# Attention and gated feed-forward on one core: the second batch's q and k loaded in runs of six tokens and transposed by TensorE

## The chip, the cores and the metric

The kernel runs on one core of a Trainium2 chip. The time is device microseconds of one execution. The kernel before was run eight times: the median is 413.78 us, the lowest 411.63, the highest 416.57.

A core has five engines that work side by side, each through its own instructions in order. TensorE (PE) multiplies matrices out of SBUF into PSUM, VectorE (DVE) and ScalarE (ACT) read PSUM and compute element by element, GpSimd (POOL) computes on SBUF and here also issues nearly all loads, and SyncE (SP) issues DMA transposes and stores.

## What is computed

There are 8 batches, 8 heads, 576 tokens of 64 values per head, and 16 beacon keys and values that every token may attend to. In float32:

```python
k_all = concatenate([beacon_k, k], axis=2)
v_all = concatenate([beacon_v, v], axis=2)
scores = (q @ k_all.T) / 8          # causal over k, open over the beacons
a = softmax(scores)
x = (a @ v_all)                     # to (4608 tokens, 512)
out = (gelu(x @ w_gate) * (x @ w_val)) @ w_out     # d_ff = 1536
```

## The kernel before, in words

**Batches and chunks.** The outer loop goes over the 8 batches. For each, an attention fills 576 columns of `xT_sb` (the transposed x, bf16); then a gate phase (`gate_val`) works on one chunk of 512 tokens: 12 tiles, each of 8 matmuls of 512 columns, a GELU on ACT and a product on DVE. The output product (`o(n)`, n matmuls of 512 columns) is behind by a chunk and is strewn over the next attentions to fill TensorE there. After the last batch a ninth chunk follows.

**Attention.** Heads go in four pairs. Per pair, `scores` makes the transposed scores in four chunks (S0 to S3), each of which ACT turns into exp; the scores' PSUM tile has two buffers (`psum_s`), which the gate phase uses too. `mask` clears what lies above the diagonal, on POOL (affine select) or on DVE by a table. `sums` (Z) makes the row sums and the first 64 columns of the values product, `values` (V) the rest, `invert` (I) the reciprocals on DVE, `scale` (M) writes `xT_sb`. `sums` and `values` have one PSUM buffer each, with the tags z and x; the output product has one with the tag o.

**The order is written out by hand.** `attention(b, *slots)` gets one string per slot; each word emits one step, and `keep` holds the program order on every engine. S, Z, V, I, M are as above, with the pair as the digit; `O12` is twelve matmuls of the output product; `N3` issues the next three loads of a queue (`load_next`); `aMC` and `dMC` mask chunk C of pair M on POOL or DVE; `kMt` and `qMt` transpose pair M through the PSUM bank t.

**How q and k reach TensorE.** q and k must lie transposed in `qkT` (`qk_ring`, two buffers). For batch 0, `load_runs` loads two heads of q or k with six tokens, 1.5 KB, to a piece, and `trans` makes 12 transposes on TensorE per operand and pair (plus one for the beacon keys), which DVE copies from PSUM to `qkT` in the right token order. For batches 1 to 7, `qk_loads` loads 11 row tiles with 256-byte pieces, and at the start of the gate phase before, `xbar_transpose` (lines 161 to 168) puts ten DMA transposes on SP's queue. Attention b+1 starts when they have landed.

**DMA semaphores.** In the built program the loads that POOL issues take eight semaphores in turn: each waits until the load eight places before it has landed.

Of the kernel before, what the change touches and what calls it, by code (L numbers as in the profile page):

```python
# [58 lines left out]
def kernel(  # L59
# [53 lines left out]
    def dma(out_ap, in_ap):  # L113
        keep(nc.gpsimd.dma_start(out=out_ap, in_=in_ap))  # L114

    def load_runs(h0, h1):
        for src, dst in ((q, q6), (k, k6)):
            dma(dst[:, h0:h1, :], src[0, h0:h1, :, :].rearrange("h (p r) d -> p h (r d)", r=RUN))

    def load_rows(start, dst, src, h0, h1):  # L120

# [24 lines left out]
    def qk_loads(b):  # L146

        qt, kt = q_ring[b % 2], k_ring[b % 2]

        def rows(dst, src):  # L150
            return dst.rearrange("p (h d) -> p h d", d=D), src.rearrange("h p d -> p h d")

        loads = [rows(kt[0:NB, 0, :], beacon_k[b])]
        for j in range(5):
            r0, n = (NB, 112) if j == 0 else (0, KROWS[j])
            loads.append(rows(kt[r0 : r0 + n, j, :], k[b, :, S_LO[j] : S_LO[j] + n, :]))
            n = min(P, S - j * P)
            loads.append(rows(qt[0:n, j, :], q[b, :, j * P : j * P + n, :]))
        return loads

    def xbar_transpose(b):
        qt, kt, qkT = q_ring[b % 2], k_ring[b % 2], qk_ring[b % 2]
        for j in range(5):
            n = KROWS[j]
            keep(nc.sync.dma_start_transpose(out=qkT[:, 1, :, j * P : j * P + n], in_=kt[0:n, j, :]))  # L165
            n = P if j < 4 else 64
            c = NB + j * P
            keep(nc.sync.dma_start_transpose(out=qkT[:, 0, :, c : c + n], in_=qt[0:n, j, :]))  # L168
# [4 lines left out]
    def load_v(b):  # L173
        dst = flat(v_ring[b % 2])
        load_beacon(dma, dst[0:NB, 0, :], beacon_v[b])
        load_keyed(dma, dst, v[b], 0, H)
# [12 lines left out]
    def load_out_w():  # L189
        dma(wo_sb, moe_w_out.rearrange("(ii p) m -> p ii m", p=P))  # L190
# [24 lines left out]
        n = in_ap.shape[0]  # L215
        keep(nc.tensor.transpose(out_ap, in_ap, ident[0:n, 0:n]))

    def trans(m, w, t_ps, copies):

        src = (q6, k6)[w]  # L220
        if w:
            tr(t_ps[:, S : S + NB], bk0[:, m * P : (m + 1) * P])
        by_run = t_ps[:, 0:S].rearrange("p (r t) -> p r t", r=RUN)
        for r in range(RUN):
            for hi in range(2):
                tr(by_run[64 * hi : 64 * hi + 64, r, :], src[:, 2 * m + hi, r * D : (r + 1) * D])
        dst = qk_ring[0]
        if w:
            copies[0][1](dst[:, 1, m, 0:NB], t_ps[:, S : S + NB])
        c0 = 0  # L230
        for c1, copy in copies:
            copy(
                dst[:, w, m, NB + c0 : NB + c1].rearrange("p (t r) -> p t r", r=RUN),
                t_ps[:, 0:S].rearrange("p (r t) -> p t r", r=RUN)[:, c0 // RUN : c1 // RUN, :],
            )
            c0 = c1
# [4 lines left out]
    def act_copy(o, i):  # L241
        keep(nc.scalar.copy(o, i))

    def trans_in(tag, m, w, copy=None):
        t_ps = bank(tag, BF16, 1024, "t_ps")
        trans(m, w, t_ps, [(S, copy or dve_copy)])

    exp_of, x_of, z_of = {}, {}, {}

    def scores(b, m, *chunks):  # L250
        i = b * NPAIR + m
        qkT = qk_ring[b % 2]
        for c in chunks:
            if c == 0:
                exp_of[i] = epool.tile([P, 2, EXP_W], BF16, name="expT", tag="expT")
            expT = exp_of[i]
            s_ps = psum_s.tile([P, 2, 512], FP32, name="s_ps", tag="s")
            for t, s_lo, w, col in CHUNKS[c]:
                for hi in range(2):
                    r = slice(64 * hi, 64 * hi + 64)  # L260
                    mm(
                        s_ps[:, hi, col : col + w],
                        qkT[r, 1, m, t * P : (t + 1) * P],
                        qkT[r, 0, m, NB + s_lo : NB + s_lo + w],
                        True,
                        True,
                    )
            o, w = CHUNK_OFF[c], CHUNK_W[c]
            act(expT[:, :, o : o + w], s_ps[:, :, 0:w], ACT.Exp, scale=QK_SCALE)
            if b:  # L270
                mask(b, m, c)

    def mask(b, m, c, by_table=False):
# [110 lines left out]
    def gate_val(ci, f0, f1):  # L384
        for fi in range(f0, f1):
            gate_val_mms(ci, fi, range(K_CHUNKS))
            gate_val_end(ci, fi)
# [13 lines left out]
    def o(n):  # L401
        for _ in range(n):
            ci, u = divmod(out_done[0], OUT_UNITS)
            ti, fi = divmod(u, F_TILES)
            if fi == 0:
                o_ps_of[0] = psum_o.tile([P, D_MODEL], FP32, name="o_ps", tag="o")
            o_ps = o_ps_of[0]
            mm(
                o_ps,
                h_of[ci][:, fi, ti * P : (ti + 1) * P],  # L410
                wo_sb[:, fi, :],
                fi == 0,
                fi == F_TILES - 1,
            )
            if fi == F_TILES - 1:
                o_sb = opool.tile([P, D_MODEL], FP32, name="o_sb", tag="o_sb")
                keep(nc.vector.tensor_copy(o_sb, o_ps))  # L417
                n0 = ci * CH + ti * P
                keep(nc.sync.dma_start(out=out[n0 : n0 + P, :], in_=o_sb))
            out_done[0] += 1  # L420
# [7 lines left out]
    def attention(b, *slots, extra=None):  # L428


        for m, slot in enumerate(slots):
            for step in slot.split():
                kind, n = step[0], step[1:]
                if kind == "S":
                    scores(b, m, *(int(c) for c in n))
                elif kind == "Z":
                    sums(b, int(n or m - 1))
                    if not n:
                        invert(b, m - 1)
                elif kind == "I":  # L440
                    invert(b, int(n))
                elif kind == "V":
                    values(b, int(n or m - 1))
                    if not n:
                        scale(b, m - 1)
                elif kind == "M":
                    scale(b, int(n))
                elif kind == "O":
                    o(int(n))
                else:  # L450
                    extra[kind](*n) if kind in "kqrwLhyad" else extra[kind](n)

# [1 line left out]

    exp_table()
    heat(8)
    load_runs(0, 2)
    load_beacon(dma, bk0, beacon_k[0])
    keep(
        nc.gpsimd.affine_select(  # L460
# [6 lines left out]
            channel_multiplier=1,  # L467
        )
    )
    load_runs(2, 4)  # L470
    keep(
        nc.gpsimd.affine_select(
            out=tri,
# [7 lines left out]
    )  # L481
    for w, copies, n in ((0, [(S, dve_copy)], 0), (1, [(114, act_copy), (S, act_copy)], 1)):
        t0 = psum_s.tile([P, 2048], BF16, name="t0_ps", tag="s")
        trans(0, w, t0, copies)
        heat(n)

    queue = []
# [1 line left out]
    def load_next(n):  # L489
# [2 lines left out]

    W_CUT = ((0, 512), (512, 1024), (1024, 1536))
    extra = {
        "k": lambda m, tag: trans_in(tag, int(m), 1),
        "q": lambda m, tag: trans_in(tag, int(m), 0),
        "a": lambda m, c: mask(0, int(m), int(c)),
        "d": lambda m, c: mask(0, int(m), int(c), by_table=True),
        "r": lambda m: load_runs(2 * int(m), 2 * int(m) + 2),
        "h": lambda n, tag: heat(int(n), tag),  # L500
        "L": lambda: load_out_w(),
        "y": lambda t: load_v_tile(0, int(t)),
        "X": lambda n: load_v(1),
        "N": lambda n: load_next(int(n)),
        "w": lambda i: load_gate_val(*W_CUT[int(i)]),
    }
    queue.extend(qk_loads(1))
    attention(
        0,
        "r2 h3x S0 k1o q1x S1 r3 y2 S2 d00 y0 q2o y1 k2x S3 d02 y3 d01 d03", "S0 y4 S1 w0 Z0 d10 S2 I0 a11 S3 k3x", "a12 S0 q3o S1 S2 a13 V0 M0 Z1 V1 w1 S3", "a21 I1 a20 a23 M1 S0 S1 a22 w2 Z2 V2 I2 S2 S3", "h3o a30 a31 a32 M2 a33 Z3 V3 I3 M3",  # L510
        extra=extra,
    )
    load_next(99)
    load_v(1)
    gelu_table()
    gate_val_first(0, heat, 2, 1)
    xbar_transpose(1)
    gate_val(0, 1, F_TILES)

    for b in range(1, B):  # L520
        exp_table()
        if b + 1 < B:
            queue.extend(qk_loads(b + 1))
        if b == 1:
            attention(b, "L S0 S1 S2 S3 N3", "S0 S1 Z0 S2 I0 S3 V0 N3", "M0 Z1 S0 S1 O7 I1 S2 S3 V1 M1 N3", "S0 S1 Z2 V2 S2 I2 S3 M2 O5 N2", "Z3 I3 V3 M3 O12", extra=extra)
        elif b == 2:
            attention(b, "S0 O12 S1 S2 O12 S3 N3", "S0 Z0 S1 S2 I0 O12 S3 V0 M0 N3", "S0 S1 Z1 V1 S2 S3 O7 N3", "S0 I1 S1 M1 Z2 V2 S2 S3 I2 M2 N2", "O1 O4 Z3 V3 I3 O12 M3", extra=extra)
        else:
            attention(b, "O5 S0 S1 O7 S2 S3 O2 N3", "S0 S1 Z0 I0 V0 S2 M0 S3 O10 N3", "S0 S1 Z1 V1 I1 S2 S3 M1 O12 N3", "S0 S1 Z2 V2 I2 M2 S2 S3 O5 N2", "Z3 I3 V3 M3", extra=extra)
        gelu_table()  # L530
        if b + 1 < B:
            load_next(99)
            load_v(b + 1)
        gate_val_first(b, o, 0 if b == 1 else 0 if b == 2 else 7)
        if b + 1 < B:
            xbar_transpose(b + 1)
        gate_val(b, 1, F_TILES)
# [35 lines left out]
```

## Time and profile before

| | us |
|---|---|
| median of 8 runs | 413.78 |
| the profiled execution's own time | 413.64 |
| its span | 411.9 |
| PE busy (94% of the span) | 387.3 |
| DVE / ACT / POOL busy | 190.9 / 189.2 / 167.9 |

The stages of the first batches, by the chain and the timeline of the profile (us from the span's start):

| stage | start | end |
|---|---|---|
| attention 0 (first scores to first gate matmul) | 7.25 | 28.87 |
| gate phase 0 | 28.87 | 50.69 |
| attention 1 | 50.69 | 78.68 |
| gate phase 1 | 78.68 | 99.49 |
| attention 2 | 99.49 | 124.58 |

From batch 3 on each batch takes 42.8 us. In the profile, L195 is the helper of all matmuls, L198 of all activations, L114 of all loads, L286 the mask on POOL, L165 and L168 the DMA transposes of k and q, L216 the transposes on TensorE, L239 their copies on DVE. PEclk is the granted TensorE clock as a part of full speed.

### The profile page before, as it was taken

To read this page: it belongs to the slowest core of one execution; us is meant where nothing else is said; L and a number is where in the kernel's file an instruction comes from. 1 tells how busy PE (TensorE), PEld (TensorE's weight loads), DVE (VectorE), ACT (ScalarE), POOL (GpSimd) and SP (SyncE) were. 2 spreads that over 40 slices of the span, in tenths; PEclk is the share of its full clock that TensorE was granted. 3 is DMA by queue.
4 is the path that set the end of the run, shared out by engine and by line. 5 is a ranking of instruction groups with operands and counts; after the bars stand their busy time and mean duration, and the time that the engine had idled before them with its cause. 6 is when DMAs were issued, how large, how long until landed. Compare 5 with 4: busy or idle time off the path is not lost.

```text
span 411.9 us, 6523 instructions
## 1 busy us (share of the span) xinstructions
PE 387.3 (94%) x2565; PEld 176.6 (43%) x2565; DVE 190.9 (46%) x326; ACT 189.2 (46%) x255; POOL 167.9 (41%) x301
## 2 busy tenths in 40 slices
PE   7889939999999999999999999999999999999975
PEld 3444314444444444444444344444444444444432
DVE  2673305643474446543664366436634574333321
ACT  3743347335662386337643665357434853312200
POOL 8769229800693049603970198009910420000000
PEclk9789969999999999999999999999999999999999
DMA  7999999990699329960999099918991100001012
GB/s 99 181 184 152 159 156 64 124 148 9 102 108 146 66 36 128 123 110 28 103 131 130 24 98 108 147 27 98 110 150 39 53 28 25 0 27 51 27 52 76
DMA packets 151983, 37.38 MB, mean 91 GB/s; under 512 B 141200, under 2 KB 147344, under 8 KB 151952
## 3 DMA queue, kind: packets, MB, share of 16 engines
q0 software_dynamic: 111824, 19.15, 61.1%
q1 hardware_dynamic: 40128, 17.82, 20.6%
q8 instruction: 20, 0.33, 0.3%
q14 instruction: 11, 0.09, 0.1%
HBM read 38.27 MB, written 9.44 MB: 116 GB/s over the span
## 4 chain that ended last, share of the span: by engine, by line
PE 78%; POOL 6%; DMA 5%; SPq 3%; DVE 3%; issue 2%; ACT 2%; POOLq 0%; DVEq 0%
PE gv_ps L195 40%; PE o_ps L195 21%; PE s_ps L195 6%; PE z_ps L195 6%; PE x_ps L195 5%; DMA qkT<-q_sb 3%; POOL expT L286 2%; DVE o_sb L417 2%; ACT expT L198 2%; SPq L165 2%; DMA k_sb<-in_k_dram 2%; SPq L168 1%; DMA v_sb<-in_v_dram 1%; POOL k_sb L114 1%; POOL q_sb L114 1%
## 5 line engine op out<-in xcount | busy, mean ns | idle before, releaser
L198 ACT ACTIVATE ge_sb<-gv_ps 128x512 bf16<-128x512 f32 x108 | 64.5, 597 | 157.4 <-PE gv_ps L195 157.4
L379 DVE TENSOR_TENSOR hT_sb<-gv_ps,ge_sb 128x512 bf16<-128x512 f32 x108 | 74.7, 692 | 118.0 <-ACT ge_sb L198 118.0
L286 POOL TENSOR_SCALAR_AFFINE_SELECT expT<-expT 128x256 bf16<-128x256 bf16 (+2 forms) x154 | 56.2, 396 | 163.7 <-ACT expT L198 163.5
L198 ACT ACTIVATE expT<-s_ps 128x1024 bf16<-128x1024 f32 (+3 forms) x128 | 103.4, 861 | 41.2 <-PE s_ps L195 38.8
L195 PE MATMUL gv_ps<-xT_sb,wg_sb 128*128 128x512 bf16 x432 | 112.2, 379 | 0.5 <-DVE xT_sb L347 0.5
L195 PE MATMUL gv_ps<-xT_sb,wv_sb 128*128 128x512 bf16 x432 | 112.2, 379 | 0.0
L195 PE MATMUL o_ps<-wo_sb,hT_sb 128*128 128x512 bf16 x432 | 103.5, 380 | 4.0 <-DVE o_sb L417 3.8
L195 PEld LDWEIGHTS <-wv_sb 128*128 128x128 bf16 x432 | 42.3, 98 | 51.8 <-issue 1.1
L195 PEld LDWEIGHTS <-wg_sb 128*128 128x128 bf16 x432 | 41.8, 98 | 51.1 <-issue 1.6
L195 PEld LDWEIGHTS <-hT_sb 128*128 128x128 bf16 x432 | 39.9, 98 | 52.3 <-issue 7.1
L195 PE MATMUL s_ps<-qkT 64*128 64x80 bf16 (+5 forms) x384 | 41.7, 294 | 10.1 <-DMA qkT<-q_sb 6.8
L417 DVE COPY o_sb<-o_ps 128x512 f32<-128x512 f32 x36 | 24.8, 690 | 44.0 <-PE o_ps L195 44.0
L330 DVE STREAM_TRANSPOSE zt<-z_ps 128x576 f32<-128x576 f32 x32 | 25.1, 783 | 41.6 <-PE z_ps L195 41.6
L114 POOL DMA_DIRECT2D v_sb<-in_v_dram x40 | 34.0, 888 | 0.8 <-DMA q_sb<-in_q_dram 0.8
L195 PE MATMUL z_ps<-expT,ones 80*64 80x80 bf16 (+5 forms) x384 | 31.6, 296 | 1.8 <-DVE xT_sb L347 1.4
L195 PEld LDWEIGHTS <-qkT 64*128 64x128 bf16 x384 | 14.8, 96 | 43.0 <-issue 36.0
L114 POOL DMA_DIRECT2D k_sb<-in_k_dram x35 | 29.9, 854 | 1.7 <-DMA wv_sb<-in_moe_w_val_dram 0.9
L114 POOL DMA_DIRECT2D q_sb<-in_q_dram x35 | 30.2, 863 | 0.2
L195 PE MATMUL x_ps<-expT,v_sb 128*64 128x512 bf16 (+4 forms) x320 | 28.8, 311 | 0.0
L335 DVE STREAM_TRANSPOSE rec<-rz 128x576 f32<-128x576 f32 x32 | 24.9, 778 | 1.1
L347 DVE TENSOR_TENSOR xT_sb<-x_ps,rec 128x512 bf16<-128x512 f32 x32 | 21.8, 682 | 3.1 <-PE x_ps L195 3.1
L195 PEld LDWEIGHTS <-ones 128*64 128x64 bf16 (+1 forms) x384 | 16.2, 113 | 15.6 <-issue 8.8
(36 smaller groups left out, 105.2 us busy)
## 6 DMA issues: line engine op xcount, KB each, us to landing
out_dram<-o_sb SPq DMA_DIRECT2D x36, 256.0 KB, 2.4
q_sb<-in_q_dram POOLq DMA_DIRECT2D x28, 128.0 KB, 4.5
v_sb<-in_v_dram POOLq DMA_DIRECT2D x24, 128.0 KB, 5.7
k_sb<-in_k_dram POOLq DMA_DIRECT2D x21, 128.0 KB, 4.9
wg_sb<-in_moe_w_gate_dram POOLq DMA_DIRECT2D x3, 512.0 KB, 6.7
wv_sb<-in_moe_w_val_dram POOLq DMA_DIRECT2D x3, 512.0 KB, 8.5
wo_sb<-in_moe_w_out_dram POOLq DMA_DIRECT2D x1, 1536.0 KB, 18.2
v_sb<-in_v_dram POOLq DMA_DIRECT2D x8, 112.0 KB, 3.7
```

The costliest lines, as they stand in the source:

```text
L114: keep(nc.gpsimd.dma_start(out=out_ap, in_=in_ap))
L165: keep(nc.sync.dma_start_transpose(out=qkT[:, 1, :, j * P : j * P + n], in_=kt[0:n, j, :]))
L168: keep(nc.sync.dma_start_transpose(out=qkT[:, 0, :, c : c + n], in_=qt[0:n, j, :]))
L195: keep(nc.tensor.matmul(out_ap, lhsT, rhs, start=start, stop=stop, **kw))
L198: keep(nc.scalar.activation(out_ap, in_ap, func, **kw))
L286: nc.gpsimd.affine_select(out=d, in_=d, pattern=[[0, 2], [1, DIAG[t]]], compare_op=ALU.is_ge, fill=0.0, base=base, channel_multiplier=-1,)
L330: keep(nc.vector.transpose(zt, z_of[i][:, Z0 : Z0 + S]))
L335: nc.vector.transpose(rec.rearrange("p (n j) -> p n j", j=32), rz.unsqueeze(2).to_broadcast([P, NBLK, 32]))
L347: nc.vector.tensor_tensor(out=xT_sb[:, m, b * S + q0 : b * S + q1], in0=acc[:, 0 : q1 - q0], in1=rec[:, q0:q1], op=ALU.mult,)
L379: nc.vector.tensor_tensor(out=h_of[ci][:, fi, :], in0=gv_ps[:, 1, :], in1=ge_sb, op=ALU.mult)
L417: keep(nc.vector.tensor_copy(o_sb, o_ps))
```

## The change

Batch 1 gets its q and k as batch 0 does. Its loads are `load_runs` pieces (eight, and the beacon keys into `bk0`) instead of eleven row tiles. `xbar_transpose(1)` is gone from gate phase 0. Pair 0 is transposed on TensorE inside gate phase 0: k after tile 6 through the bank z, q after tile 7 through the bank x. Pairs 1 to 3 are transposed inside attention 1. There, the masks are now written out, three chunks of pair 0 on DVE and the rest on POOL. The 24 matmuls of the output product in attention 1 stand at its end (`O12` twice) instead of as `O7`, `O5`, `O12`. Of batch 2's eleven loads three are issued early in attention 1 and eight behind its last mask. `load_v(1)` and `load_out_w()` stand behind gate phase 0 in the program; in POOL's own order they still follow batch 1's q and k loads. Attention 2 keeps its 60 matmuls of the output product, with its steps and loads in another order.

```diff
-    def load_runs(h0, h1):
-        for src, dst in ((q, q6), (k, k6)):
-            dma(dst[:, h0:h1, :], src[0, h0:h1, :, :].rearrange("h (p r) d -> p h (r d)", r=RUN))
+    def runs(b, m):
+        h = slice(2 * m, 2 * m + 2)
+        return [
+            (dst[:, h, :], src[b, h, :, :].rearrange("h (p r) d -> p h (r d)", r=RUN))
+            for src, dst in ((q, q6), (k, k6))
+        ]
+
+    def load_runs(b, m):
+        for out_ap, in_ap in runs(b, m):
+            dma(out_ap, in_ap)
...
-    def trans(m, w, t_ps, copies):
+    def trans(b, m, w, t_ps, copies):
...
-        dst = qk_ring[0]
+        dst = qk_ring[b]
...
-            if b:
+            if b > 1:
                 mask(b, m, c)
...
-    queue.extend(qk_loads(1))
+    queue.extend(runs(1, 0) + [by_token(bk0, beacon_k[1])])
+    for m in range(1, NPAIR):
+        queue.extend(runs(1, m))
...
     load_next(99)
-    load_v(1)
     gelu_table()
     gate_val_first(0, heat, 2, 1)
-    xbar_transpose(1)
-    gate_val(0, 1, F_TILES)
+    gate_val(0, 1, 7)
+    trans_in("z", 1, 0, 1)
+    gate_val(0, 7, 7 + 1)
+    trans_in("x", 1, 0, 0)
+    gate_val(0, 7 + 1, F_TILES)
+    load_v(1)
+    load_out_w()
...
-            attention(b, "L S0 S1 S2 S3 N3", "S0 S1 Z0 S2 I0 S3 V0 N3", "M0 Z1 S0 S1 O7 I1 S2 S3 V1 M1 N3", "S0 S1 Z2 V2 S2 I2 S3 M2 O5 N2", "Z3 I3 V3 M3 O12", extra=extra)
+            attention(b, "S0 S1 k1x a01 q1z S2 k3o d00 S3 d03 d02", "S0 N3 k2o S1 a11 a10 Z0 q2o I0 S2 a12 V0 M0 S3 a13", "S0 S1 q3o a21 Z1 I1 a20 S2 V1 a22 S3 M1", "S0 a23 S1 a30 a31 Z2 S2 I2 V2 a32 M2 S3 a33 O12", "Z3 N3 V3 I3 M3 N3 O12", extra=extra)
         elif b == 2:
-            attention(b, "S0 O12 S1 S2 O12 S3 N3", "S0 Z0 S1 S2 I0 O12 S3 V0 M0 N3", "S0 S1 Z1 V1 S2 S3 O7 N3", "S0 I1 S1 M1 Z2 V2 S2 S3 I2 M2 N2", "O1 O4 Z3 V3 I3 O12 M3", extra=extra)
+            attention(b, "S0 O12 N3 S1 S2 O12 S3 N3", "S0 Z0 I0 S1 S2 O12 S3 V0 N3", "S0 S1 M0 Z1 V1 I1 S2 S3 O7", "S0 S1 M1 Z2 V2 I2 S2 S3 N2 M2", "O2 O3 Z3 I3 V3 M3 O12", extra=extra)
```

More of the change, by code (lines that the diff above doesn't have):

```diff
@@ L114, in dma, with by_token @@
         keep(nc.gpsimd.dma_start(out=out_ap, in_=in_ap))
[L116 to L118 removed]
+    def runs(b, m):
[7 more added lines that the diff above has]
+            dma(out_ap, in_ap)
+    def by_token(dst, src):
+        return dst.rearrange("p (h d) -> p h d", d=D), src.rearrange("h p d -> p h d")
     def load_rows(start, dst, src, h0, h1):
@@ L148, in qk_loads @@
         qt, kt = q_ring[b % 2], k_ring[b % 2]
-        def rows(dst, src):
-            return dst.rearrange("p (h d) -> p h d", d=D), src.rearrange("h p d -> p h d")
-        loads = [rows(kt[0:NB, 0, :], beacon_k[b])]
+        loads = [by_token(kt[0:NB, 0, :], beacon_k[b])]
         for j in range(5):
             r0, n = (NB, 112) if j == 0 else (0, KROWS[j])
-            loads.append(rows(kt[r0 : r0 + n, j, :], k[b, :, S_LO[j] : S_LO[j] + n, :]))
+            loads.append(by_token(kt[r0 : r0 + n, j, :], k[b, :, S_LO[j] : S_LO[j] + n, :]))
             n = min(P, S - j * P)
-            loads.append(rows(qt[0:n, j, :], q[b, :, j * P : j * P + n, :]))
+            loads.append(by_token(qt[0:n, j, :], q[b, :, j * P : j * P + n, :]))
         return loads
@@ L242, in act_copy, with trans_in @@
         keep(nc.scalar.copy(o, i))
-    def trans_in(tag, m, w, copy=None):
+    def trans_in(tag, b, m, w):
         t_ps = bank(tag, BF16, 1024, "t_ps")
-        trans(m, w, t_ps, [(S, copy or dve_copy)])
+        trans(b, m, w, t_ps, [(S, dve_copy)])
     exp_of, x_of, z_of = {}, {}, {}
@@ L449, in attention @@
                     o(int(n))
+                elif kind in "adkq":
+                    extra[kind](b, *n)
                 else:
@@ L456 @@
     heat(8)
-    load_runs(0, 2)
+    load_runs(0, 0)
     load_beacon(dma, bk0, beacon_k[0])
@@ L469 @@
     )
-    load_runs(2, 4)
+    load_runs(0, 1)
     keep(
@@ L483 @@
         t0 = psum_s.tile([P, 2048], BF16, name="t0_ps", tag="s")
-        trans(0, w, t0, copies)
+        trans(0, 0, w, t0, copies)
         heat(n)
@@ L494 @@
     extra = {
[L495 to L499, printed above, removed]
+        "k": lambda b, m, tag: trans_in(tag, b, int(m), 1),
+        "q": lambda b, m, tag: trans_in(tag, b, int(m), 0),
+        "a": lambda b, m, c: mask(b, int(m), int(c)),
+        "d": lambda b, m, c: mask(b, int(m), int(c), by_table=True),
+        "r": lambda m: load_runs(0, int(m)),
         "h": lambda n, tag: heat(int(n), tag),
-        "L": lambda: load_out_w(),
         "y": lambda t: load_v_tile(0, int(t)),
-        "X": lambda n: load_v(1),
         "N": lambda n: load_next(int(n)),
```

## The prediction

> **What bounds the kernel now.** I read the chain of work that ended last first, in order of time. From batch 3 on it is TensorE nearly alone, 42.8 us per batch. Between gate phase 0 and attention 1 it leaves TensorE:
>
> ```profile
> 46.40 1.19 SPq L165
> 47.70 10.35 DMA qkT<-q_sb
> 58.09 0.60 PE s_ps L195 x6
> 58.71 1.81 ACT expT L198 x2
> ```
>
> The ten DMA transposes go out from 34.63 us on, one per 1.4 us, and the last needs 10.35 us to land, beside the load of `wo_sb`. TensorE's timeline shows the hole (start, length, what, and in brackets the idle time before):
>
> ```profile
> 49.66 1.03 PE L195 MATMUL gv_ps<-xT_sb,wv_sb 128*128 128x512 bf16 x4
> 54.23 0.61 PE L195 MATMUL s_ps<-qkT 64*128 64x512 bf16 x2 [3.55 <-DMA qkT<-q_sb]
> 58.09 0.97 PE L195 MATMUL s_ps<-qkT 64*128 64x64 bf16 x8 [3.25 <-DMA qkT<-q_sb]
> 59.73 0.36 PE L195 MATMUL s_ps<-qkT 64*128 64x208 bf16 x2 [0.67 <-ACT expT L198]
> ```
>
> TensorE ends at 50.69, and the second scores start at 58.09: 7.4 us with only 0.6 of work. The clock tells the rest. It changes only at multiples of 3.41 us (near 16.05, 22.88, 53.59 and 63.83), so I asked for busy time by stage in stretches of that length, for TensorE (PE busy, instructions, granted clock, then DMA), and for the transposes on TensorE alone (the first busy column):
>
> ```profile
> 9.22:12.64 3.42, 2.82 (x60) 1.00 1.63 157
> 12.64:16.05 3.41, 1.92 (x31) 1.00 2.13 165
> 16.05:19.46 3.41, 3.24 (x30) 0.50 1.25 204
> 19.46:22.88 3.42, 3.42 (x32) 0.50 1.23 202
> ...
> 57.00:60.42 3.42, 1.33 (x10) 0.50 0.95 157
> 60.42:63.83 3.41, 3.26 (x28) 0.50 0.15 13
> 63.83:67.24 3.41, 2.57 (x36) 1.00 1.12 71
> ```
>
> ```profile
> 9.22:12.64 3.42, 1.24 (x38) 2.98 (x6) 0.00 (x0) 1.00 1.63 157
> 12.64:16.05 3.41, 0.55 (x13) 0.00 (x0) 0.00 (x0) 1.00 2.13 165
> 16.05:19.46 3.41, 0.69 (x12) 1.51 (x3) 0.00 (x0) 0.50 1.25 204
> ```
>
> A stretch 1.92 us busy is followed by half the clock, one 2.57 us busy is not. After the hole the half clock lasts from 53.59 to 63.83. So the wait costs 6.8 us of idle and slows attention 1, which ends at 78.68: 28.0 us for 24 output matmuls at 0.216 us (5.2) and four pairs of exp.
>
> **What the change removes.** The wait for `qkT` goes: no DMA transposes of batch 1 remain (SP has ten fewer). The runs land in time. POOL reaches them at 27.8; eight at 0.69 us and the beacon keys at 0.56 are issued in 6.1 us instead of 9.2. Before, the ninth load waited until 34.4 for the last weights, and the new ninth waits too; pair 0 is issued by 29 and needed near 43. The v loads and `wo_sb` follow earlier than before, and `wo_sb` (43.3, 18.2 us to land) is first read later than now.
>
> **What it adds to gate phase 0.** The groups give a transpose of q a mean of 244 ns and of k 210. A hundred at these means would be 23 us, but the starts overlap: at full clock twelve follow each other in 0.38 us, with the beacon keys 0.47. [...] The row has the pace, so pair 0 costs 0.85 us of TensorE, all on the path: the gate phase ends at 51.5. On DVE a gate tile is 0.69 of product and 1.03 idle; each copy (0.75, for k 0.15 more) stands behind a product and fits the idle time. If it did not, the two buffers of `gv_ps` would hold TensorE; at worst that is one copy, 0.75.
>
> **Attention 1 at full clock, by rows.** The table load after the last GELU ends at 52.62 now, at 53.5 then; four exps of a pair take 3.24.
> Slot 0: exps 53.5 to 56.7; the second scores wait for the last product, near 52.9.
> Slot 1: exps of S0 and S1 to 58.6. DVE has copies of k1, q1, k3 and three masks (0.28 each) until 57.3; Z0 waits for these masks and runs to 58.2, q2 to 58.6, S2 to 58.8. Exps end at 60.1.
> Slot 2: exps of S0 and S1 to 62.0, but Z1 needs the bank z: the q2 copy (0.75), inverses (1.85) and the first scale (0.22) from 58.6 give 61.45. Z1 to 62.3, S2 to 62.5, exps end at 64.0.
> Slot 3: DVE ends the scales at 62.1, the q3 copy at 62.9, inverses and first scale at 65.0; Z2 to 65.9; exps end at 67.5.
> Tail: O12 from 66.9 to 69.5, Z3 0.86, V3 0.69, O12 2.6: gate phase 1 starts at 73.6, 5.1 us earlier than 78.68. POOL is not late: 17 masks at 0.4 and three loads are under 10 us.
>
> **The clock speaks against this sum.** From 51.5 to 57.3 TensorE has five scores groups and five groups of transposes. By the rows (0.35 to 0.39 a scores group, 0.45 a transposing one, ends modelled as in the view) a 3.41 us stretch of it is about 2.1 busy: between the 1.92 that lost the clock and the 2.57 that kept it, nearer the first. [...] I take the drop, near 55 to 57.
>
> Its price: attention 0's half clock lasted two stretches, 6.8 us. Half of that, 3.4, is lost where TensorE is never idle; in the sum above it is idle about a fifth, so 2.7 (three stretches: 5.1 less 1.2, near 3.9). With 2.7 gate phase 1 starts at 76.3, a gain of 2.4; with 3.9 the gain is 1.2; with none 5.1.
>
> **What moves behind it.** Batch 2's last eight loads (0.74 to 0.9 each, some 7 us) follow the last mask on POOL and end about 1.5 us after gate phase 1 has started; they ended 2.2 before it, and the v loads follow. SP's first transpose comes 1.4 after the start anyway (80.11, behind the store of the last output tile) and takes one load per 1.3 us; the ten went out until 93.6, DMA is idle from 96, and attention 2 began at 99.49. So 3.5 us of slack cover this; gone, each microsecond late is one of TensorE, after an O12 of 2.6 that stands before S1.
>
> Attention 2, now 25.1 us, has 60 x 0.216 = 13.0 of output matmuls and about 9 of attention work, so at most 3.1 can go. Near its end the chain runs through POOL: three loads (116.6 to 119.3), masks, then Z3 at 1.43 instead of 0.91; and the gate's last k chunk waits 0.22 for `xT_sb`. The new order puts the loads a slot earlier and the last scale before O12. The first three now stand ahead of S1's masks, but sums wait for S3's mask in any case (106.94), so nothing excludes either sign: -1 to 3.1. I take 0.8, from 0.5 for Z3, 0.2 for the wait and a little from POOL. Batches 3 to 7 do not change.
>
> The sum on the profiled execution: 413.64 - 2.4 - 0.8 = 410.4; the median of the runs is 0.14 above that execution, which I leave out.
>
> **The rivals.**
> - The clock holds. For: 2.1 is not 1.92, and the stretches' phase may cover gate work. [...] 413.64 - 5.1 - 0.8 = 407.7. Chance 0.22.
> - The gain is given back: three slow stretches and nothing in attention 2, 413.64 - 1.2 = 412.4. [...] Chance 0.13.
> - Slower: the half clock holds until the output matmuls. All of them now stand at the end, where before an O7 stood in slot 2. The place is slots 1 to 3: at half clock Z is 1.60 and V 1.48, so Z2 starts near 68.4 and exps end at 72.6; the first O12 at half clock takes 5.2, from 71.9, to about 77; Z3 and V3 at full clock and O12 end at 81.2 at most, 80.1 if the clock wakes inside the first O12. Gate phase 1 starts 1.4 to 2.5 late: 415.0 to 416.1, say 415.4. It decides if no stretch before 69 wakes the clock. Against: two busy stretches sufficed at 16.05. Chance 0.10.
> That the DMA transposes stay is excluded by the built program's order.
>
> The forecast, 410.4, has the remaining 0.55; alone it spans 409.2 to 412.0 (gains of 1.2 to 2.7 and 0.4 to 1.7). The range of 407.2 to 413.0 takes in the clock that holds and the gain given back. About 0.5% (2.1 us) is what a measurement here tells from no change: faster is under 411.7. That is 0.48 of the forecast and all of the first rival, 0.70; same 0.23 (0.07, the second rival, and 0.03 of the third, whose near end lies within the bound); slower 0.07, the rest of the third.
>
> **What would show it.** In the profile after: no wait of scores for a DMA after gate phase 0; that phase 0.85 longer; a granted clock of 0.5 for two or three stretches from near 55; first gate matmul of phase 1 near 76; attention 2 about 24.3 us long; from there 42.8 per batch. I am wrong if the clock stays at 1.00 (time near 407.7), if scores of attention 2 wait for `qkT`, or if `x_ps` or `z_ps` buffers stop TensorE longer than DVE's rows say.

## The result, and the profile after

The changed kernel takes 408.1 us, the median of 11 runs (406.44 to 409.36), against 413.81 us, the median of 32 runs of the kernel before (411.14 to 416.57). The ratio is 0.9865, with a 95% interval of 0.9844 to 0.9887: a gain of 5.7 us, or 1.1 to 1.6%. The profiled execution of the changed kernel took 406.44 us, its span 404.7. That is as short as the fastest of the 11 runs and 1.7 below their median, which matters below.

In the new profile L202 is the helper of the matmuls (L195 before), L205 of the activations, L223 the transposes on TensorE, L246 their copies on DVE and L386 the product of the gate phase.

First, the chain of work that ended last in the changed kernel, in order of time (start, length, what), from pair 0's transposes of k to gate phase 1:

```profile
39.97 0.13 PE t_ps L223 x6
40.09 1.83 PE gv_ps L202 x8
41.93 0.38 PE t_ps L223 x12
42.30 7.03 PE gv_ps L202 x32
...
49.97 1.28 ACT L430
51.25 0.01 issue
51.26 2.73 ACT expT L205 x3
...
57.19 0.76 DVE qkT L246
57.95 0.70 DVE zt L337
...
58.98 0.79 DVE rec L342
...
60.62 0.76 DVE qkT L246
...
70.22 2.69 PE o_ps L202 x12
72.91 3.24 PE gv_ps L202 x15
```

No SyncE and no DMA is left between gate phase 0 and attention 1. The table load of ACT (L430), three exps and then DVE lead instead. The same stretch in TensorE's timeline:

```profile
48.29 1.03 PE L202 MATMUL gv_ps<-xT_sb,wv_sb 128*128 128x512 bf16 x4
49.25 0.39 PE L202 MATMUL s_ps<-qkT 64*128 64x512 bf16 x2
50.73 0.39 PE L202 MATMUL s_ps<-qkT 64*128 64x64 bf16 x6 [1.09 <-DVE hT_sb L386]
...
52.34 0.37 PE L202 MATMUL s_ps<-qkT 64*128 64x464 bf16 x2 [0.48 <-ACT expT L205]
```

The second scores come 1.5 us after the first instead of 3.9; what holds them is the product on DVE that frees the second scores buffer, for 1.09 us. Third, stretches of 3.41 us (length, PE busy, granted clock, then DMA), with the boundaries of this run's own clock changes:

```profile
48.52:51.93 3.41, 2.24 (x37) 1.00 0.58 97
51.93:55.34 3.41, 2.43 (x42) 1.00 0.01 2
55.34:58.75 3.41, 3.41 (x38) 0.50 1.13 75
58.75:62.17 3.42, 3.03 (x50) 1.00 0.13 7
```

The clock is halved (0.50) for one stretch of attention 1. Before, it was halved for three (53.59 to 63.83).

I set the two profiled executions side by side by the starts of TensorE's groups. Attention 1 is counted here from the start of the last matmul group of gate phase 0 to the first gate matmul of phase 1, attention 2 from its first scores to the last k chunk of its first gate tiles (the last quarter of the contraction, which needs the last columns of `xT_sb`, so that the wait for them is in it):

| stage | before | after | shorter by |
|---|---|---|---|
| attention 0, to the first gate matmul | 28.87 | 26.43 | 2.44 |
| gate phase 0, to its last group | 20.79 | 21.86 | -1.07 |
| attention 1 | 29.02 | 24.46 | 4.56 |
| attention 2 | 26.77 | 25.86 | 0.91 |
| span | 411.9 | 404.7 | 7.2 |

The rest, about 0.4, lies behind the last copy on DVE, at the very end: 3.30 us from there to the end of the span before, 2.92 after. It is no chance of one run: the five profiles with batch 1's DMA transposes have 3.3 to 3.4 there, the nine with transposes on TensorE 2.9 to 3.0. Why is open. The 2.44 is not the change's: attention 0 has the same code in both. Over the fourteen profiled executions of this study its end lies anywhere from 26.4 to 29.0 us, with no, one, two or three stretches of half clock in it. So the change itself shows 4.8 us in the profile: 4.56 - 1.07 + 0.91 + 0.4.

### The profile page after: what moved, and what is told of

Its sections match the earlier page's. It is cut to its first block, busy times and chain, and to the rows that moved or that the text cites. A ratio compares the mean times of both kernels' runs of the same rounds, so it can differ in the third digit from the quotient of the medians.

```text
span 404.7 us, 6704 instructions
## 1 busy us (share of the span) xinstructions
PE 387.2 (96%) x2665; PEld 178.1 (44%) x2665; DVE 197.6 (49%) x341; ACT 188.9 (47%) x255; POOL 163.5 (40%) x296
## 4 chain that ended last, share of the span: by engine, by line
PE 89%; DVE 5%; ACT 2%; DMA 1%; issue 1%; POOL 1%; POOLq 0%; DVEq 0%
PE gv_ps L202 46%; PE o_ps L202 24%; PE s_ps L202 7%; PE z_ps L202 7%; PE x_ps L202 5%; DVE o_sb L424 2%; ACT expT L205 2%; DMA k<-in_k_dram 1%; DVE rec L342 1%; DVE zt L337 1%; PE t_ps L223 1%; DVE xT_sb L354 1%; DVE qkT L246 1%; DVE rz L339 0%; POOL q L114 0%
## 5 line engine op out<-in xcount | busy, mean ns | idle before, releaser
L205 ACT ACTIVATE ge_sb<-gv_ps 128x512 bf16<-128x512 f32 x108 | 64.5, 597 | 159.0 <-PE gv_ps L202 159.0
L386 DVE TENSOR_TENSOR hT_sb<-gv_ps,ge_sb 128x512 bf16<-128x512 f32 x108 | 74.7, 692 | 118.0 <-ACT ge_sb L205 118.0
L293 POOL TENSOR_SCALAR_AFFINE_SELECT expT<-expT 128x256 bf16<-128x256 bf16 (+2 forms) x151 | 55.2, 394 | 159.8 <-ACT expT L205 145.7
L205 ACT ACTIVATE expT<-s_ps 128x1024 bf16<-128x1024 f32 (+3 forms) x128 | 103.1, 862 | 32.6 <-PE s_ps L202 29.8
L202 PE MATMUL gv_ps<-xT_sb,wg_sb 128*128 128x512 bf16 x432 | 112.3, 379 | 0.3 <-DVE xT_sb L354 0.3
L202 PE MATMUL gv_ps<-xT_sb,wv_sb 128*128 128x512 bf16 x432 | 112.2, 379 | 0.0
L202 PE MATMUL o_ps<-wo_sb,hT_sb 128*128 128x512 bf16 x432 | 103.3, 380 | 4.0 <-DVE o_sb L424 3.8
L202 PEld LDWEIGHTS <-wv_sb 128*128 128x128 bf16 x432 | 42.3, 98 | 51.5 <-issue 0.6
L202 PEld LDWEIGHTS <-wg_sb 128*128 128x128 bf16 x432 | 41.6, 98 | 50.8 <-issue 1.6
L202 PEld LDWEIGHTS <-hT_sb 128*128 128x128 bf16 x432 | 40.0, 98 | 52.3 <-issue 6.9
L202 PE MATMUL s_ps<-qkT 64*128 64x80 bf16 (+5 forms) x384 | 41.0, 286 | 5.3 <-ACT expT L205 3.9
L202 PE MATMUL z_ps<-expT,ones 80*64 80x80 bf16 (+5 forms) x384 | 30.4, 294 | 0.8 <-DVE xT_sb L354 0.5
L202 PEld LDWEIGHTS <-qkT 64*128 64x128 bf16 x384 | 14.6, 94 | 37.1 <-issue 33.7
L202 PE MATMUL x_ps<-expT,v_sb 128*64 128x512 bf16 (+4 forms) x320 | 28.0, 305 | 0.0
L114 POOL DMA_DIRECT2D k_sb<-in_k_dram x30 | 25.7, 857 | 0.8 <-DMA out_dram<-o_sb 0.3
L114 POOL DMA_DIRECT2D q_sb<-in_q_dram x30 | 25.8, 862 | 0.2
L342 DVE STREAM_TRANSPOSE rec<-rz 128x576 f32<-128x576 f32 x32 | 24.9, 778 | 1.1
L202 PEld LDWEIGHTS <-ones 128*64 128x64 bf16 (+1 forms) x384 | 15.4, 113 | 13.2 <-issue 7.5
```

Source lines behind the costliest of these rows:

```text
L202: keep(nc.tensor.matmul(out_ap, lhsT, rhs, start=start, stop=stop, **kw))
L205: keep(nc.scalar.activation(out_ap, in_ap, func, **kw))
L293: nc.gpsimd.affine_select(out=d, in_=d, pattern=[[0, 2], [1, DIAG[t]]], compare_op=ALU.is_ge, fill=0.0, base=base, channel_multiplier=-1,)
L342: nc.vector.transpose(rec.rearrange("p (n j) -> p n j", j=32), rz.unsqueeze(2).to_broadcast([P, NBLK, 32]))
L386: nc.vector.tensor_tensor(out=h_of[ci][:, fi, :], in0=gv_ps[:, 1, :], in1=ge_sb, op=ALU.mult)
```

## The experiments

The theory after the two profiles were compared: the gain is the wait for `qkT`, and one stretch of half clock is what remains to be had. Its rivals: the wait could have been taken away without TensorE's transposes; the order of attention 2 carries part of it; and the clock does not see transposes, so it must drop whatever the order (an assumption, which two runs below put to the test). "Gate + attention 1" below is the time from the first gate matmul of phase 0 to that of phase 1, 49.81 before and 46.32 after. Ratios are to the kernel before, run on the same chip. Each version was executed four to ten times, and the intervals of all versions of the changed kernel overlap the changed kernel's own. So the times tell none of them from the changed kernel; what is said of their stages rests on one profiled execution each.

### Idle matmuls in attention 1

The edit adds heat matmuls, whose result is not used, to slot 0 (`h3o` is three of them, in the bank o):

```diff
-"S0 S1 k1x a01 q1z S2 k3o d00 S3 d03 d02"
+"S0 h3o S1 k1x a01 q1z h2o S2 k3o d00 S3 h2o d03 d02"
```

> The kernel after, with seven idle matmuls of 512 columns (0.216 us each) put into slot 0 of attention 1, where TensorE waits. From the start of the last gate matmul group of phase 0 to the first gate matmul of phase 1 the kernel after took 24.5 us (48.29 to 72.75) with one 3.41 us stretch at half clock. Theory (the half clock costs time): the clock stays at 1.00 through attention 1 and this time falls by about 1.4 us to 23.1; the whole to about 406.7. Rival (ScalarE and VectorE set the pace, so the half clock is free): the clock stays at 1.00 and the time stays at 24.5 or grows by what the idle matmuls delay.

Measured: 406.44 us, ratio 0.9831 (0.9785 to 0.9877). The clock stayed at 1.00 and attention 1 took 24.01, between the theory (23.1) and the rival (24.5). But the last idle group stood 0.66 us behind a DVE copy that held the bank o, so the price of the half clock was not read cleanly. The edit was therefore made again with the last group in the bank x:

```diff
+"S0 h3o S1 k1x a01 q1z h2o S2 k3o d00 S3 h2x d03 d02"
```

> The kernel after, with idle matmuls in slot 0 of attention 1 as in the first such run, but the last group goes through the PSUM bank x, which is free, and not through the bank o, where it waited 0.66 us for a copy and made the first sums 0.7 us late. Theory (a stretch at half clock costs more than the 0.45 us seen, because that delay hid part of it): from the last gate matmul group of phase 0 to phase 1 about 23.4 us, against 24.46 in the kernel after with one stretch at half clock; the whole 1.0 below the kernel after where its clock fell once. Rival (VectorE's chain of copies, inverses and scales paces slots 1 to 3, the half clock is nearly free): 24.0.

Measured: 406.92 us, ratio 0.9841 (0.9796 to 0.9886), clock 1.00, attention 1 23.38. One stretch at half clock costs 24.46 - 23.38 = 1.1 us in this place. The run with attention 2 in its old order, below, has the same steps in attention 1 and again one such stretch; there attention 1 took 24.75, so the price is 1.1 in one execution and 1.4 in the other. As a time for the kernel this is not a resolved gain.

### Idle transposes: does the clock see them?

The same three places, but with 12, 8 and 8 transposes of the 128x128 identity on TensorE (`T`), result not used:

```diff
+"S0 T12 S1 k1x a01 q1z T8 S2 k3o d00 S3 T8 d03 d02"
```

> The same places, filled with 28 idle transposes of 128 by 128 on TensorE in place of the idle matmuls (about 1.5 us of it in all). Theory (transposes do not count as busy for the clock gate): half clock stays in attention 1, one stretch or more, and the time from the last gate group to phase 1 is 24.5 or up to 1 us longer. Rival (all TensorE work counts): the clock stays at 1.00 and it is near 23.1, as with idle matmuls.

Measured: 407.47 us, ratio 0.9843 (0.9786 to 0.9899). The clock stayed at 1.00 in attention 1, which took 24.01, against the theory. Then once more with transposes of the kernel's own shape, 96x64, 28, 18 and 18 of them:

```diff
-        tr(t[:, 0:P], ident)
+        tr(t[0:D, 0 : S // RUN], q6[:, 0, 0:D])
...
+"S0 T28 S1 k1x a01 q1z T18 S2 k3o d00 S3 T18 d03 d02"
```

> Transposes whose result is not used are added to slot 0 of attention 1, at the same three places as in the run with 128x128 ones, but in the kernel's own shape, 96x64: 28, 18 and 18, which at 0.38 us for twelve is about the same busy time (0.9, 0.6, 0.6). If transposes of this shape count in full for the clock, it stays at 1.00 through attention 1, which takes about 24.0 as it did with the large ones (24.46 without any). If they do not count, or count by their smaller size, one stretch at half clock stays and attention 1 takes 24.5 to 25.2.

Measured: 408.75 us, ratio 0.9879 (0.9854 to 0.9904). Two tables of this run, in stretches of 3.41 us: all of TensorE, then only the tile of the idle transposes (length, PE busy, clock, DMA):

```profile
52.08:55.49 3.41, 3.41 (x84) 1.00 0.00 0
55.49:58.91 3.42, 2.69 (x57) 1.00 0.24 20
58.91:62.32 3.41, 3.19 (x52) 1.00 1.00 64
```

```profile
52.08:55.49 3.41, 2.08 (x46) 1.00 0.00 0
55.49:58.91 3.42, 0.95 (x18) 1.00 0.24 20
```

The kernel's own transposes take another 1.01 and 0.91 in these two stretches. So of 3.41 us busy only 0.3 was matmul in the first, and of 2.69 only 0.8 in the second, and the clock stayed at 1.00 through both and after. In the changed kernel a stretch of 2.43 busy, with 1.3 of it matmul, was enough to lose it. So transposes of this shape count as busy, at least in part; that they count in full is not shown. Attention 1 took 24.70 all the same: the idle groups were longer than I had meant (the 28 took 1.31), and the last one stood 0.73 behind a DVE copy. So the clock decides between the theories here; the stage's time does not.

### Attention 2 in its old order

The changed kernel with the slots of attention 2 of before:

```diff
+attention(b, "S0 O12 S1 S2 O12 S3 N3", "S0 Z0 S1 S2 I0 O12 S3 V0 M0 N3", "S0 S1 Z1 V1 S2 S3 O7 N3", "S0 I1 S1 M1 Z2 V2 S2 S3 I2 M2 N2", "O1 O4 Z3 V3 I3 O12 M3", extra=extra)
```

> The kernel after, with the step order of attention 2 taken from the kernel before. Theory (the reorder gives about 0.9 us by moving loads away from the masks and the last scale ahead of the output matmuls): from the first scores of attention 2 to its second k-chunk gate group 26.8 us in place of 25.9, with Z of pair 3 near 1.43 us and a wait for xT_sb of 0.2; the whole about 409.0. Rival (attention 2 is bound by the number of output matmuls): 25.9 stays.

Measured: 408.08 us, ratio 0.9864 (0.9817 to 0.9912), so nothing that the times can resolve. In the profile attention 2 took 25.84 to its first gate matmul instead of 25.52, and the gate's last k chunk waited 0.22 for `xT_sb` again. From the last group of gate phase 1 to that last k chunk it is 27.51 against 26.82: the order is worth 0.7 us of the 0.91.

### Pair 0 transposed at the start of attention 1

Gate phase 0 runs without transposes, and pair 0 comes first in attention 1:

```diff
-    gate_val(0, 1, 7)
-    trans_in("z", 1, 0, 1)
-    gate_val(0, 7, 7 + 1)
-    trans_in("x", 1, 0, 0)
-    gate_val(0, 7 + 1, F_TILES)
+    gate_val(0, 1, F_TILES)
...
+"k0z q0x S0 S1 k1z a01 q1x S2 k3o d00 S3 d03 d02"
```

> The kernel after, with pair 0 transposed at the start of attention 1 and not inside gate phase 0. Theory: gate phase 0 is 1.07 us shorter, but the first scores wait for VectorE's two copies behind the last product: they start 3.1 us after the gate matmuls and the first exp near 3.4, in place of 1.9 behind the table load. Net 0.4 to 1 us slower than the kernel after. Rival (the copies are hidden behind the table load): 0.2 to 1 us faster.

Measured: 408.93 us, ratio 0.9889 (0.9844 to 0.9935). Gate phase 0 became 1.07 shorter, attention 1 2.23 longer. TensorE's timeline of this run has the new wait:

```profile
52.88 0.60 PE L202 MATMUL s_ps<-qkT 64*128 64x512 bf16 x8 [2.08 <-DVE qkT L246]
```

The scores now stand behind two DVE copies, and the clock is halved for two stretches (54.9 to 61.8) instead of one. Inside the gate phase the transposes cost 1.07, with the copies beside it; here they cost twice that. How much of the 2.23 is the wait for the copies and how much the second stretch at half clock is not separated.

### The kernel before with its clock kept up

Heat matmuls in the hole of the kernel before, which still waits for its DMA transposes:

```diff
-"L S0 S1 S2 S3 N3"
+"L h9o h7o S0 h9o h5o S1 S2 S3 N3"
```

> The kernel before, with idle matmuls in the two holes before attention 1's first and second scores (16 and 14, some 3.5 and 3.0 us), so that the wait for the DMA transposes stays and the clock does not fall. Theory (the wait itself is most of the cost, the half clock after it about 2 us): the second scores still start near 58, the part from there to phase 1 falls from 20.6 to about 18.6, the whole is near 411.8. Rival 1 (the wait alone counts): no change, 413.8. Rival 2 (the half clock is most of the cost): 409 or less.

Measured: 413.01 us, ratio 0.9985 (0.9951 to 1.0019): no change that can be told. The clock stayed at 1.00, and the second scores still waited for the last DMA transpose, which took 10.30 us to land. From the second scores to gate phase 1 it took 19.85 us against 20.59: the half clock had cost the kernel before only 0.74 and not the 2 that were expected, and the hole itself was the rest. A second thing is to be seen. In this run attention 0 ended 2.25 us earlier than in the profile of before (26.62 against 28.87), but the second scores started only 0.85 earlier (57.24 against 58.09). If the DMA transposes follow the loads and not the gate phase, the kernel before would give most of a fast attention 0 away in its wait and the changed kernel would keep it, which would explain why the medians differ by 5.7 where the stages show 4.8. It is not shown. The last two runs of the next section, both with DMA transposes and the same steps up to there, point the other way: their attention 0 ended 1.71 apart (26.63 and 28.34), their first scores in attention 1 started 2.32 apart (51.05 and 53.37). And the times of the kernel before are not spread less than those of the changed one: a standard deviation of 1.2 us over 32 executions against 1.1 over 11.

### The weights' load out of the way of the DMA transposes

The kernel before, with only the 1.5 MB load of `wo_sb` (`L`) moved behind S1:

```diff
-"L S0 S1 S2 S3 N3"
+"S0 S1 L S2 S3 N3"
```

> The kernel before, with the load of the output weights issued after the second scores of attention 1 and not behind the v loads. Theory (the last DMA transpose took 10.35 us to land because it shares the DMA engines with that 1.5 MB load): it lands in 4 to 5 us, the second scores start near 53, some 5 us earlier; the output weights then land near 67 to 70 and the first seven output matmuls wait up to 4 us, so the whole is 410 to 413. Rival (the transposes are slow in themselves): the second scores start near 58 as before, and the whole is 414 or more.

Measured: 417.17 us, ratio 1.0082 (1.0059 to 1.0105): slower. TensorE's timeline of this run says why:

```profile
53.05 0.74 PE L195 MATMUL s_ps<-qkT 64*128 64x512 bf16 x8 [2.23 <-DMA qkT<-k_sb]
...
68.96 1.44 PE L195 MATMUL o_ps<-wo_sb,hT_sb 128*128 128x512 bf16 x3 [6.17 <-DMA wo_sb<-in_moe_w_out_dram]
```

The two waits of 3.55 and 3.25 for `qkT` became one of 2.23, so it was the load beside them that made the DMA transposes land late; nothing else was moved. But the first output matmuls, in slot 2, now waited 6.17 for their weights. The next experiment takes that wait away as the change did, by moving the output matmuls to the end of attention 1, and keeps the DMA transposes:

```diff
-"L S0 S1 S2 S3 N3", "S0 S1 Z0 S2 I0 S3 V0 N3", "M0 Z1 S0 S1 O7 I1 S2 S3 V1 M1 N3", "S0 S1 Z2 V2 S2 I2 S3 M2 O5 N2", "Z3 I3 V3 M3 O12"
+"S0 L S1 S2 S3 N3", "S0 S1 Z0 S2 I0 S3 V0 N3", "M0 Z1 S0 S1 I1 S2 S3 V1 M1 N3", "S0 S1 Z2 V2 S2 I2 S3 M2 N2 O12", "Z3 I3 V3 M3 O12"
```

> The kernel before, with DMA transposes kept: the load of the output weights goes out behind the first scores of attention 1, and the 24 output matmuls of attention 1 stand at its end, in two twelves, as in the changed kernel. One theory: most of the gain is the removed wait, and that wait was the DMA transposes beside the weights' load; then the second scores start 3.3 us after the last group of gate phase 0 (as in the earlier run with the late load), the weights land by 69, before the first O12, gate phase 0 stays at 20.8, attention 1 takes 24.0 to 25.3 from the last group to phase 1 (24.46 in the changed kernel), and the time is 408 to 410. Rival: the transposes on TensorE are needed for it: the weights are late for the first O12 or the clock stays halved for three stretches, attention 1 takes 27 or more, and the time is 411 or more.

Measured: 408.96 us, ratio 0.9907 (0.9871 to 0.9943). In the chain of waits of this run the transposes still stand, but shorter:

```profile
43.10 1.67 SPq L168
...
44.89 6.18 DMA qkT<-k_sb
51.07 0.39 PE s_ps L195 x2
...
66.24 2.70 PE o_ps L195 x12
68.94 0.98 PE z_ps L195 x13
```

The DMA that TensorE waits for takes 6.18 us and not 10.35, the weights are there before the first O12 at 66.2, and gate + attention 1 takes 46.51, 0.2 more than in the changed kernel. The clock is halved for two stretches (51.4 to 58.3). With attention 2 in the new order as well, by the diff of the section on its old order read the other way:

```diff
-"S0 O12 S1 S2 O12 S3 N3", "S0 Z0 S1 S2 I0 O12 S3 V0 M0 N3", "S0 S1 Z1 V1 S2 S3 O7 N3"
+"S0 O12 N3 S1 S2 O12 S3 N3", "S0 Z0 I0 S1 S2 O12 S3 V0 N3", "S0 S1 M0 Z1 V1 I1 S2 S3 O7"
```

> The run before this one but two (DMA transposes kept, the weights' load behind the first scores, the output matmuls at the end of attention 1), and now attention 2 in the changed kernel's order too: everything of the change but the runs and the transposes on TensorE. If those bring nothing by themselves, gate phase 0 and attention 1 together take 46.5 again (46.3 in the changed kernel), attention 2 falls from 26.0 to about 25.5, and the time is 408.0 to 408.7, with an interval that holds the changed kernel's ratio of 0.9865. If they do bring something beside the removed contention, it stays at 409 or above.

Measured: 408.96 us again, ratio 0.9914 (0.9884 to 0.9945). Attention 2 fell to 25.53 and lost its 0.21 for `xT_sb`, as expected; but the scores waited longer for `qkT` (the last transpose was issued at 47.52, 1.35 later than in the other run), and gate + attention 1 took 47.58:

```profile
53.37 0.70 PE L195 MATMUL s_ps<-qkT 64*128 64x512 bf16 x8 [3.22 <-DMA qkT<-k_sb]
```

So the expectation of 408.0 to 408.7 was missed by a little, on the side of the rival. By the ratios, 0.93% and 0.86% of the 1.35% (3.8 and 3.6 us) come with the DMA transposes in place. In the second run this includes the order of attention 2, which is 0.9 us in its profile. So the load that no longer lies beside the transposes, with output matmuls that can wait for it, brings 3.8 us by the one run and about 2.7 by the other. The second run has everything of the change but the runs of tokens and the transposes on TensorE. These bring what is left, 2.0 us or about a third, by taking out the last 2 to 3 us of wait for 1.07 in the gate phase; 0.4 of it is the shorter end. Both intervals still overlap the changed kernel's (0.9844 to 0.9887), and by the stages the share is 0.2 us against the one run (46.51 and 46.32) and 1.3 against the other (47.58), so that third is likely and not sharp.

### Output matmuls in the thin slot

Twelve of attention 2's output matmuls are put into slot 0 of attention 1, with the output weights loaded ahead of the v tiles. All the work stays. The expectation speaks of other banks for pairs 1 to 3 in a general way; in the kernel as it ran, k of pairs 1, 2 and 3 all go through the bank x.

```diff
+"S0 O5 S1 k1x a01 q1z O3 S2 k3x d00 S3 d03 d02 O4", "S0 N3 k2x S1 a11 a10 Z0 q2o I0 S2 a12 V0 M0 S3 a13"
...
+"S0 O12 N3 S1 S2 O12 S3 N3", "S0 Z0 I0 S1 S2 O12 S3 V0 N3", "S0 S1 M0 Z1 V1 I1 S2 S3", "S0 S1 M1 Z2 V2 I2 S2 S3 N2 M2", "Z3 I3 V3 M3 O12"
```

> The kernel after, with twelve output matmuls moved from attention 2 into the gaps of attention 1's slot 0 (five, three and four), the output weights loaded ahead of the v tiles, and k of pairs 1, 2 and 3 transposed through z, x and x or as far as the banks allow. It does the same work. Theory: the gaps of 1.09, 0.48 and 0.57 us hold most of the 2.6 us, the clock stays at 1.00, attention 2 is 2.0 to 2.6 us shorter: about 2 us below the kernel after, near 406. Rival (the output weights or the bank o are late, or attention 2 is not bound by its output matmuls): the gain of attention 2 is under 1 us or attention 1 grows by as much.

Measured: 406.68 us, ratio 0.9839 (0.9789 to 0.989). Attention 1 took 23.82 at full clock, with twelve matmuls (2.6 us) more in it. That is 0.44 above the 23.38 of the run with seven idle ones, so the thin slot hides most of them. But attention 2, with 2.6 us less work, fell by 0.55 only. Its timeline shows where the rest went:

```profile
109.56 0.79 PE L202 MATMUL s_ps<-qkT 64*128 64x512 bf16 x8 [0.80 <-ACT expT L205]
...
113.56 0.91 PE L202 MATMUL z_ps<-expT,ones 128*64 128x64 bf16 x12 [1.27 <-DVE xT_sb L354]
```

So another place was emptied, the second O12 of slot 0:

```diff
+"S0 O12 N3 S1 S2 S3 N3", "S0 Z0 I0 S1 S2 O12 S3 V0 N3", "S0 S1 M0 Z1 V1 I1 S2 S3 O7", "S0 S1 M1 Z2 V2 I2 S2 S3 N2 M2", "O2 O3 Z3 I3 V3 M3 O12"
```

> As the run that moved twelve output matmuls from attention 2 into slot 0 of attention 1, but in attention 2 it is the second twelve of slot 0 that goes, and the seven and the two and three near the end stay. If the new waits of that run (0.8 for ACT, 1.3 for DVE) were those of the places emptied, attention 2 falls by about 1.6 from 25.5 to 23.9 and the time is near 405.5. If attention 2 without these twelve is held by ACT and DVE whatever the place, it stays near 25.0 and the time at 406.7.

Measured: 406.22 us, ratio 0.9829 (0.9802 to 0.9856), the lowest ratio of all. Attention 2 took 24.78, and the waits only moved:

```profile
97.78 0.27 PE L202 MATMUL s_ps<-qkT 64*128 64x208 bf16 x2 [0.87 <-ACT expT L205]
98.61 0.39 PE L202 MATMUL s_ps<-qkT 64*128 64x512 bf16 x2 [0.57 <-ACT expT L205]
```

With 48 output matmuls attention 2 is held by ACT and DVE near 24.9 whichever place is emptied. This version is the best median here, but its interval overlaps the changed kernel's.

## Why the prediction was right in its sign and short in its size

The time, 408.1, lies inside the range (407.2 to 413.0), 2.3 below the forecast of 410.4 and close to the rival in which the clock holds (407.7). What happened stands between the two: the clock dropped, once. That the median lies so near the rival is partly luck: 0.9 us of the gain stands in no stage of the two profiles.

**The bound and what is removed: right.** The wait for `qkT` went whole, 6.8 us of idle, and no DMA wait of scores is left after gate phase 0. The view that carried this was the chain, with its 10.35 us of landing. What the prediction did not ask is whether that landing could have been shortened; it named the load of `wo_sb` beside it, and moving that load and the matmuls that need it brought 2.7 to 3.8 of the 5.7 us.

**Gate phase 0: right in kind, 0.2 short.** Predicted +0.85, measured +1.07. The sum took the pace of back-to-back starts, 0.38 for twelve; the rows of the changed kernel show gaps of 0.58 and 0.48 between the gate groups around the two steps. One by one, at the groups' mean durations (244 and 210 ns), pair 0's 25 would be a quarter of the prediction's 23 us, 5.7, so the row was the right one to take.

**The full-clock sum of attention 1: right.** On the table's measure it is 23.1 (from 50.5 to 73.6). The run with idle matmuls that kept the clock took 23.38. The waits stand where the sum had them: Z0 starts 5.84 after the gate phase's end, where the sum had 5.8, and then DVE's copies, transposes and scales set the pace of slots 1 to 3.

**The clock: the step that was off.** The prediction took two stretches, 2.7 us, with 3.9 for three. It was one stretch of 1.1 us. What was off is the count. The two were taken over from attention 0, and no run with the changed kernel's steps in attention 1 shows two there. That the clock would drop at all, at 0.78 by the chances, was the author's estimate; the profile of before does not show it, and the prediction's own rows do not give it: five groups of scores at 0.35 to 0.39 and five of transposes at 0.45 in the 5.8 us from 51.5 to 57.3 are 2.4 busy in 3.41 us, where it has 2.1. The changed kernel shows 2.24, after which the clock held, and 2.43, after which it fell. Since 2.4 is nearer to the 2.57 that had kept the clock than to the 1.92 that had lost it, that the clock fell at all is in part luck. The next stretch, from 55.34, was 3.41 busy (2.73 without transposes), and the clock woke at once. The price of one stretch, 1.35, was about right: 1.1 and 1.4 in the two executions that show it. It is less than the 1.7, half of 3.41, that a TensorE never idle would lose; from 57.19 on the chain runs through DVE, whose copy of q takes 0.76 at half clock (57.19) and at full clock (60.62) alike, so part of TensorE's loss lies beside it. In the kernel before, the half clock behind the second scores (58.09 to 63.83) cost 0.74 of the 2.9 us that are half of that time. The sum with the measured terms is 5.1 less 0.2 for the gate phase less 0.3 for the full-clock sum less 1.1, which gives 3.5; the table has 4.56 - 1.07 = 3.49.

**Whether transposes count as busy.** Two rows of the profile before seemed to say that they do not: 3.24 busy, 0.69 of it transposes, did not wake the clock, and 3.26 without transposes did. Those two stand too close to each other to carry it, and a row that the prediction does not show speaks against it. First all of TensorE, then the tile of the transposes alone:

```profile
5.81:9.22 3.41, 2.39 (x40) 1.00 1.20 156
```

```profile
5.81:9.22 3.41, 1.17 (x34) 1.00 1.20 156
```

Here the clock held on 1.2 of matmul, less than the 1.4 (1.92 less 0.55) of the stretch from 12.64 to 16.05, which lost it. The stretch with only 0.3 us of matmul that kept the clock decides it: for keeping the clock, transposes of this shape count, at least in part. For waking it the runs lean the other way in part. Three stretches at half clock, from the run with attention 2 in the new order and DMA transposes, from that with the weights' load moved alone, and from that with attention 2 in its old order:

```profile
17.49:20.90 3.41, 2.99 (x26) 0.50 1.24 204
11.84:15.26 3.42, 2.91 (x26) 0.50 2.34 158
15.09:18.50 3.41, 3.28 (x41) 0.50 1.36 190
```

The first, without transposes, woke the clock; the second, without them too, did not; the third, 1.50 of it transposes, did not either, though it was the busiest of the three. Others are 3.03, 3.22 and 3.26 without transposes, which woke it, 3.02 (1.29 of it transposes) and 3.30 (1.50), which did not, and 3.25 (0.58) and 3.33 (0.88), which did. How much a transpose counts for waking stays open.

**Attention 2: right.** 0.8 predicted, 0.91 measured, 0.7 of it in the order (0.9 in the pair of runs with DMA transposes). The slack for batch 2's loads held: they were issued until 73.7 and their DMA transposes until 89.0, and attention 2 started at 93.57 with no wait for `qkT`. Batches from 3 on take 42.8 as before.

**What was not in the sum.** The 0.4 us at the end of the span is in none of its terms. And the predicted time was set against one execution of before whose attention 0 happened to have two slow stretches. Where the remaining 0.9 us between 5.7 and 4.8 lie is open: the profile of the changed kernel is one of its fastest executions, that of before an ordinary one, and that the kernel before hides a fast attention 0 in its wait was argued above and is not borne out by the other runs.

## What to carry to other kernels

When the chain ends in a transfer, ask first what lies beside that transfer: here a 1.5 MB load of weights that could be needed later made ten small DMA transposes late, and moving it, together with its users, gave about half to two thirds of the gain of the whole change. Moved without its users it made the kernel 0.8% slower. Price a halved clock by what stands on the chain in that stretch: where VectorE or ScalarE leads, part of TensorE's slowdown lies beside the path; here 1.1 to 1.4 of 1.7 us reached it in one kernel and 0.74 of 2.9 in the other. And filling a thin slot with real work pays only if the slot it is taken from was not already held by another engine: here 2.6 us less of matmuls shortened attention 2 by 0.55 and 0.74, held by ScalarE and VectorE.

## What the runs showed of the hardware

- Transposes on TensorE count as busy for keeping the granted clock, at least in part: 2.08 idle and 1.01 used ones in a stretch of 3.41 us, with 0.3 of matmul, kept it at 1.00; so did 128x128 ones (2.75 busy, 1.0 of it matmul).
- How busy a stretch of 3.41 us was does not alone say whether the clock is kept. In the nine profiles in which the clock changed, every full-clock stretch that was 2.5 or more busy kept it, from attention 0 on. Below that it goes both ways: 1.27, 1.92, 2.25, 2.33 and 2.43 were followed by half clock, while 1.43 (the weights' load moved alone), 1.94 and 1.95 (DMA transposes, output matmuls at the end) and 2.24 (the changed kernel) were not. What else decides is open.
- Waking took most of a stretch: without transposes 2.99 did it and 2.91 did not; with 1.50 of transposes not even 3.30 did. The ends of matmuls are modelled, so differences of a few hundredths say little.
- The same code of attention 0 met no to three slow stretches from run to run and so ended between 26.4 and 29.0 us.
- Twelve 96x64 transposes that fill both halves of a PSUM tile in turn took 0.38 us; 28 that write one half, all to the same columns, took 1.31, 47 ns each against 32. The cause was not tried.
